# Attention feeding a four-expert MoE: x operands of a token group kept in SBUF for all experts, operand sums of the second product made in place just in time, chunks paired across token halves

## The chip, the cores and the metric

The kernel runs on one core of a Trainium2 chip, in fp32 throughout. The metric is device time in microseconds (us) of one execution. A few runs are timed, and one more execution is taken by the hardware profiler: the profile, the trace and all lines shown below come from that one execution.

## The reference

Lightning attention on q, k, v of shape (B=4, H=8, S=768, D=64), then a mixture of four experts over its output. Cut to what is computed:

```python
for b in range(nb):                      # blocks of 64 tokens
    intra = np.einsum('bhic,bhjc->bhij', qb, kb) * Dmask[None]
    intra = np.einsum('bhij,bhjd->bhid', intra, vb)
    inter = np.einsum('bhid,bhde->bhie', qb * lam_pow[None], kv_state)
    out[:, :, sl] = intra + inter
    kv_state = lam_block * kv_state + np.einsum('bhsd,bhse->bhde', kb * rev_pow, vb)
x = out.transpose(0, 2, 1, 3).reshape(B * S, H * D)         # [3072, 512]
p = domain_probs / (domain_probs.sum(-1, keepdims=True) + 1e-09)
for e in range(4):
    h = np.maximum(x @ w1[e], 0.0)                          # w1[e]: [512, 1024]
    out += p[:, e:e + 1] * (h @ w2[e])                      # w2[e]: [1024, 512]
```

## The kernel before, in words

**Tiles.** The 3072 tokens are cut into 24 chunks of 128 (a chunk is one batch row b and one stretch c of its sequence), eight chunks to a group, three groups (0, 1, 2) of 1024 tokens. A unit is a pair (group, expert), twelve in all. Chunks are worked on in pairs: attention for chunks n and n + 1 is done together, and in `where` (L110) the two chunks of a pair are neighbours in the group's order, so that a pair's 256 tokens lie in the same half of the group.

**The products.** Both matrix products of a unit use the Strassen-Winograd scheme on two levels. On each level a 2x2 block product is made from seven products M1 to M7 of sums of blocks: S1 to S4 are the sums on one side, T1 to T4 those on the other (`A_OF`, `B_OF`, L84 and L85). An outer product M of the first matrix product has seven inner products; for each the two operands are slices of tiles of [128, 7, 256], seven operands side by side: `ws` from w1 and `xs` from x. `first_product` (L862) issues them as matmuls at L884, adds the PSUM results on the vector engine (VectorE, DVE) or copies them on the scalar engine (ScalarE, ACT), and applies relu on ACT (L896). `second_product` (L923) multiplies the hidden blocks by tiles of w2 (L938), and DVE adds the gated result to the output accumulators (L951, L954). For the last group the second product is also nested on both levels (`nested_product` L1149, matmuls L1169). Group 0's first expert is made while attention for group 0 is still running, by `direct_product` (L1285, L1299).

**Order of the work.** The main loop (L1454 to L1527) runs over the units; for each, seven slots. Slot i interleaves the second product of M = `SEQ2[i]` of the present unit with the first product of M = `SEQ[i]` of the next unit (the list `order`, L1497), in eight steps x = 0 to 7. Slots are numbered 7 times the unit's position plus i. Everything else is put between these steps:

- `steps` are attention's pieces for groups 1 and 2, at slots given by the list `AT` (L641): loads two slots and one slot ahead, transposes on TensorE (L543) at the slot, scores (L570) at its end, the values (L606, L612, L620) at the end of the next one. L621 on copies a pair's output from PSUM (`op`) to `xT`, an SBUF tile that holds a whole group's x (ACT, L626).
- `chores` and `queue` are worked off by `pump` (L153). A chore is a piece of operand preparation on GpSimd (POOL); `tt` (L93) counts each POOL operation's size into a planned time `busy`, and `pump` starts the next chore when its planned start `free` has come. Stores of results wait in `queue` until the planned end of the sums. `until` (L173) pumps by force until something is made.
- `background` is a list of DVE sums, of which `rest` (L502) issues one after each step.

DMAs are issued almost all by SyncE (SP), whose queue is in order: an issue that waits holds all behind it. The tile framework adds the waits.

**The path of x.** When half of a group's chunks, or all of them, are in `xT`, `prepare_x` (L316) has POOL make the outer sums T1 to T4 and, for each of the seven M, `inner_x` (L205) makes four inner sums of 256 columns in a stage tile and stores the seven pieces in DRAM (`x_ops`, L185 to L187). `feed` (L789) then loads for each slot two tiles of 896 KB: `xs_in` (L797) from `x_ops` and `ws_in` (L799) from `w1_ops`; both tags of the pool `stream` have two buffers. So a group's x operands are loaded anew for each expert. For group 0 `own_x` (L1201) makes these sums on DVE, and the first use reads them from SBUF. `feed` stands at the first step of a slot (x = 0), from slot 6 on:

```python
        xs = stream.tile([P, 7, 256], FP32, name="xs_in", tag="x")
        nc.sync.dma_start(out=xs[:], in_=x_ops[g, MS.index(m)])
        ws = stream.tile([P, 7, 256], FP32, name="ws_in", tag="w")
        nc.sync.dma_start(out=ws[:], in_=w1_ops[e, MS.index(m)])
```

**The hidden sums.** When `first_product` has finished a quarter of the hidden blocks, `operands` (L672) puts its four sums S3, S1, S2, S4 into `background`, each into a new tile (`small`, a pool of `NPOOL` = 46 tiles of 2 KB per partition). In unit (0, 0) three blocks go through PSUM on the way (ACT copies, L689). `SEQ2` is M1, M2, M7, M6, M4, M5, M3, so S3 is read in the third slot, S2 in the fourth, S1 in the sixth and S4 in the seventh.

**Scaled q.** The states of attention, `kv`, are multiplied by q scaled with a decay (`qs`, DVE, L527 and L552), made beside qT.

Of the kernel before, what the change touches and what calls it, by code (L numbers as in the profile page):

```python
# [17 lines left out]
NPOOL = 46  # L18
# [3 lines left out]
def kernel(  # L22
# [36 lines left out]
    C = P  # L59
# [13 lines left out]
    stage = ctx.enter_context(tc.tile_pool(name="stage", bufs=8))  # L73
    w2pool = ctx.enter_context(tc.tile_pool(name="w2", bufs=6))
    stream = ctx.enter_context(tc.tile_pool(name="stream", bufs=2))
    opool = ctx.enter_context(tc.tile_pool(name="o", bufs=CPG))
# [13 lines left out]
    def small(name):  # L90
        return pool.tile([P, W], FP32, name=name, tag="t")

# [16 lines left out]

    def where(n):  # L110
        g, x = divmod(n, CPG)
        half, x = divmod(x, 4)
        return (2 * g + x // 2, 2 * half + x % 2) if g == LAST else (2 * g + half, x)

    def token(n):
        c, b = where(n)
        return b * S + c * C
# [3 lines left out]
    def load(n, names="qkv"):  # L121

        c, b = where(n)
        for name in names:
            x = small(f"{name}n")
# [12 lines left out]
    x_ops = dram.tile([NG, 7, P, 7, 256], FP32, name="x_ops")  # L138
# [4 lines left out]
    X_AT = {n: i for i, n in enumerate(("M1", "M7", "M6", "M4", "M5", "M2", "M3"))}  # L143
# [60 lines left out]

    def inner_x(eng, g, m, blk):  # L205
        at = {"B11": (0, 0), "B12": (0, 1), "B21": (1, 0), "B22": (1, 1)}
        inner(eng, ("x", g, m), x_ops[g, MS.index(m)], blk, T_OPS, at)
# [103 lines left out]
    xT = consts.tile([P, 4, G], FP32, name="xT")  # L311

    b11, b21 = xT[:, 0:2, 0:W], xT[:, 2:4, 0:W]
    b12, b22 = xT[:, 0:2, W:G], xT[:, 2:4, W:G]

    def prepare_x(g):  # L316

        st = {}

        def total(name, a, b, op):  # L320
            t = stage.tile([P, 2, W], FP32, name="xo", tag="st")
            halves(t[:], a, b, op)
            st[name] = t[:]

        def ready(m, blk):
            inner_x(nc.gpsimd, g, m, blk)

        return [lambda: ready("M1", b11), lambda: ready("M2", b21)], [
            lambda: total("T1", b12, b11, ALU.subtract), lambda: ready("M5", st["T1"]),
            lambda: total("T2", b22, st["T1"], ALU.subtract), lambda: ready("M6", st["T2"]),  # L330
            lambda: total("T3", b22, b12, ALU.subtract), lambda: ready("M7", st["T3"]),
            lambda: ready("M3", b22),
            lambda: total("T4", b21, st["T2"], ALU.subtract), lambda: ready("M4", st["T4"]),
        ]
# [1223 lines left out]
```

## Time and profile before

| What | us |
|---|---|
| median of 3 runs | 1196.85 |
| all runs | 1197.26, 1188.91, 1196.85 |
| the profiled execution | 1200.69 |
| its span (first to last instruction) | 1198.9 |
| mean granted TensorE clock in it | 0.996 |
| SyncE waits at xs_in issues (L797) for matmuls L884 | 128.8 in 31 waits |
| POOL x sums: outer (xo), 16 of 512 columns twice | 11.8 + 10.0 |
| ACT copies of op to xT (L626), 24 | 12.8 |
| ACT copies up at L689, 12 | 6.9 |
| DVE qs sums, 12 and 8 | 14.4 + 6.3 |

How to read the profile: a group of instructions is "line engine operation out<-in", with the names of tiles as the program has them and the shape; "x8" is a count of instruction records, and a 128x256 fp32 matmul has two of them. In a timeline, the bracket at the end of a row is the idle time before it and what ended it. "PEclk" is the TensorE clock that was granted, 1.00 is full. The DMA share is the mean busy share of the core's 16 DMA engines. A released wait is put down to the event that came last by the profile.

The busy time of an engine that is not the bottleneck, and its idle time, cost nothing by themselves. SyncE's waits in the table are of that sort as long as what it issues lands before its reader needs it.

### The profile page before, as it was taken

To read this page: it belongs to the slowest core of one execution; us is meant where nothing else is said; L and a number is where in the kernel's file an instruction comes from. 1 tells how busy PE (TensorE), PEld (TensorE's weight loads), DVE (VectorE), ACT (ScalarE), POOL (GpSimd) and SP (SyncE) were. 2 spreads that over 40 slices of the span, in tenths; PEclk is the share of its full clock that TensorE was granted. 3 is DMA by queue.
4 is the path that set the end of the run, shared out by engine and by line. 5 is a ranking of instruction groups with operands and counts; after the bars stand their busy time and mean duration, and the time that the engine had idled before them with its cause. 6 is when DMAs were issued, how large, how long until landed. Compare 5 with 4: busy or idle time off the path is not lost.

```text
span 1198.9 us, 17951 instructions
## 1 busy us (share of the span) xinstructions
PE 1175.7 (98%) x6559; PEld 1027.4 (86%) x6559; DVE 785.8 (66%) x1327; ACT 270.3 (23%) x476; POOL 632.1 (53%) x600
## 2 busy tenths in 40 slices
PE   8999999999999989999999999999999999999998
PEld 7888888888778878888888888888788888888887
DVE  4686795577358637756865864773565566776785
ACT  3332122112111201211120120121143352241331
POOL 2883167475338900045534272726575593683884
PEclk9999999999999999999999999999999999999999
DMA  9895969999999996799997989999987666657543
GB/s 222 230 327 178 273 227 289 354 351 319 313 328 345 325 300 198 230 293 307 309 325 259 279 295 314 290 299 310 310 267 274 228 235 238 240 214 264 204 158 96
DMA packets 266760, 324.25 MB, mean 270 GB/s; under 512 B 122640, under 2 KB 208048, under 8 KB 266672
## 3 DMA queue, kind: packets, MB, share of 16 engines
q1 hardware_dynamic: 256032, 320.28, 80.4%
q10 hardware_dynamic: 10640, 2.82, 1.1%
q8 instruction: 52, 0.85, 0.3%
q14 instruction: 36, 0.29, 0.1%
HBM read 237.69 MB, written 89.54 MB: 273 GB/s over the span
## 4 chain that ended last, share of the span: by engine, by line
PE 55%; DMA 1%; DVE 1%; ACT 0%; issue 0%; DVEq 0%; SPq 0%
PE pg L884 24%; PE q L938 15%; PE pq L1169 13%; DMA xs_in<-x_ops 1%; PE op L612 0%; DVE sums L94 0%; PE pg L1169 0%; PE sp L570 0%; PE pM L1105 0%; DMA w2b<-in_moe_w_dram 0%; PE op L606 0%; PE yp L1063 0%; PE yp L1138 0%; DVE y L1086 0%; DVE hS L94 0%; DVE st L94 0%
## 5 line engine op out<-in xcount | busy, mean ns | idle before, releaser
L884 PE MATMUL pg<-xs_in,ws_in 128*128 128x256 f32 x1960 | 474.0, 382 | 12.9 <-DMA ws_in<-w_ops 10.1
L884 PEld LDWEIGHTS pg<-xs_in,ws_in 128*128 128x128 f32 x1960 | 373.9, 191 | 67.3 <-issue 14.8
L94 DVE TENSOR_TENSOR m<-pg,m 128x512 f32<-128x512 f32 x451 | 307.8, 687 | 117.8 <-PE pg L884 110.9
L938 PE MATMUL q<-w2t,hS 128*128 128x256 f32 x1024 | 243.8, 381 | 0.0
L938 PEld LDWEIGHTS q<-w2t,hS 128*128 128x128 f32 x1024 | 194.6, 191 | 27.2 <-DMA w_ops<-w2b 0.2
L954 DVE SCALAR_TENSOR_TENSOR acc<-q,gate,acc 128x256 f32<-128x256 f32 x192 | 92.3, 481 | 147.6 <-PE q L938 146.6
L938 PE MATMUL q<-w2t,m 128*128 128x256 f32 x768 | 182.1, 380 | 0.0
L938 PEld LDWEIGHTS q<-w2t,m 128*128 128x128 f32 x768 | 145.4, 190 | 19.9
L896 ACT ACTIVATE m<-m 128x512 f32<-128x512 f32 x132 | 83.0, 630 | 296.6 <-DVE m L94 296.3
L94 POOL TENSOR_TENSOR m<-m,xT 128x512 f32<-128x512 f32 x64 | 80.6, 1274 | 69.8 <-ACT m L896 52.1
L94 POOL TENSOR_TENSOR ops<-w2b 128x256 f32<-128x256 f32 x24 | 19.2, 820 | 157.3 <-DMA w2b<-in_moe_w_dram 157.3
L892 ACT COPY m<-pg 128x512 f32<-128x512 f32 x88 | 51.5, 585 | 192.6 <-PE pg L884 192.4
L94 DVE TENSOR_TENSOR sums<-pq,sums 128x256 f32<-128x256 f32 x153 | 64.2, 421 | 46.1 <-PE pq L1169 38.9
L1169 PE MATMUL pq<-acc,w2t 128*128 128x256 f32 x352 | 86.6, 379 | 0.0
L1169 PEld LDWEIGHTS pq<-acc,w2t 128*128 128x128 f32 x352 | 66.9, 190 | 9.3 <-issue 0.3
L94 POOL TENSOR_TENSOR kn<-kn,s_decay 128x512 f32<-128x512 f32 x20 | 23.6, 1182 | 90.2 <-PE kp L543 38.8
L827 ACT ACTIVATE m<-m 128x512 f32<-128x512 f32 x44 | 27.7, 630 | 128.7 <-DVE m L94 128.7
L94 DVE TENSOR_TENSOR hS<-m,m 128x512 f32<-128x512 f32 x56 | 47.0, 839 | 14.7 <-ACT m L896 14.7
L94 POOL TENSOR_TENSOR acc<-hT,hT 128x512 f32<-128x512 f32 x32 | 40.2, 1271 | 30.3 <-PE pq L1169 28.4
L94 POOL TENSOR_TENSOR w2o<-w2b 128x512 f32<-128x512 f32 x32 | 42.7, 1355 | 25.4 <-DMA across<-in_q_dram 17.9
L94 POOL TENSOR_TENSOR ops<-w1o 128x256 f32<-128x256 f32 x32 | 27.8, 887 | 32.7 <-PE pg L884 17.3
L94 DVE TENSOR_TENSOR m<-m,m 128x512 f32<-128x512 f32 x56 | 44.9, 801 | 0.0
(159 smaller groups left out, 1351.3 us busy)
## 6 DMA issues: line engine op xcount, KB each, us to landing
xs_in<-x_ops SPq DMA_DIRECT2D x70, 896.0 KB, 6.1
ws_in<-w_ops SPq DMA_DIRECT2D x70, 896.0 KB, 8.4
w2t<-w_ops SPq DMA_DIRECT2D x66, 256.0 KB, 6.8
w2t<-w_sums SPq DMA_DIRECT2D x64, 256.0 KB, 4.0
w_ops<-ops SPq DMA_DIRECT2D x28, 512.0 KB, 4.4
w2t<-in_moe_w_dram SPq DMA_DIRECT2D x48, 256.0 KB, 3.7
w2b<-in_moe_w_dram SPq DMA_DIRECT2D x32, 256.0 KB, 6.2
w_sums<-w2o SPq DMA_DIRECT2D x16, 512.0 KB, 5.8
```

Of the source, the lines that this page charges most:

```text
L94: eng.tensor_tensor(out=o, in0=a, in1=b, op=op)
L827: nc.scalar.activation(out=o[:], in_=o[:], func=AF.Relu)
L884: nc.tensor.matmul(out=p[:, j * 256:(j + 1) * 256], lhsT=ws[i][:, j * P:(j + 1) * P], rhs=xs[i], start=(fresh and j == 0), stop=True, skip ...
L892: nc.scalar.copy(out=new[at][:], in_=p[:])
L896: nc.scalar.activation(out=new[at][:], in_=new[at][:], func=AF.Relu)
L938: nc.tensor.matmul(out=p[:, s * DH:(s + 1) * DH], lhsT=h[A_OF[m]][:, c * 256 + s * P:c * 256 + (s + 1) * P], rhs=fed2[g, e, m][uu][:, c], ...
L954: nc.vector.scalar_tensor_tensor(out=o, in0=x, scalar=w, in1=o, op0=ALU.mult, op1=ALU.add)
L1169: nc.tensor.matmul(out=p[:, 0:256], lhsT=fed3[e, m, x // 2][:, x % 2, c * P:(c + 1) * P], rhs=b[B_OF[i]][:, c * 256:(c + 1) * 256], start= ...
```

## The change

**x stays in SBUF.** There are seven fixed tiles of [128, 7, 256], one for each M, in a new pool `xp`. For group 0 the attention's values are copied straight into them, and DVE makes the inner sums in place (`x_steps`). For groups 1 and 2 ACT copies a pair's output into one stage tile, POOL makes the four outer sums of the pair (`pair_sums`), and SyncE stores the pair's seven blocks in DRAM (`x_blocks`, two stores of 384 and 512 KB). Later `x_fill` loads the blocks into the seven tiles, one M per slot from slot 18 (group 1) and slot 43 (group 2), by two DMAs of 256 KB each, and a chore makes the inner sums on POOL, in place. `feed` loads only `ws_in`. `x_ops` is gone, as are `prepare_x` and `inner_x`.

**Chunks paired across halves.** So that a pair's outer sums can be made alone, `where` puts the two chunks of a pair into the two halves of the group. The output rows of a chunk pair of the last group are then 256 neighbouring tokens, and the final stores are written accordingly: `give_across` issues four DMAs after the first half and four after the second, where before all eight followed the second.

**Hidden sums in place.** `operands` queues only S3, which takes the place of A21. `later_operands`, called at the start of each slot, queues S2 in the slot of M4 (in place of S3), S1 in the slot of M2 (in place of A11) and S4 in the slot of M5 (in place of A12). `SEQ2` becomes M1, M7, M4, M6, M2, M5, M3. The copies through PSUM of unit (0, 0) are gone.

**Room and places.** q is scaled in place after the scores (in group 0 on DVE right behind the four masks). `kv` and `q_decay` come from the pool of small tiles and are given back when the last attention is done (`forget`); `gate_bc` lies in `s_decay`; in group 0 the k tiles come from the accumulators' pool and the v tiles from that of w2. `NPOOL` is 41 for 46, the stage pool has 7 tiles for 8. The end weights `w2s` of the nested products take six different x tiles. The list `AT` is 7, 10, 13, 15, 22, 27, 32, 37 for 4, 8, 13, 17, 24, 29, 34, 39. The matmuls are the same in number and shapes.

The diff, cut to its core:

```diff
-NPOOL = 46
+NPOOL = 41
...
-    stage = ctx.enter_context(tc.tile_pool(name="stage", bufs=8))
+    stage = ctx.enter_context(tc.tile_pool(name="stage", bufs=7))
     w2pool = ctx.enter_context(tc.tile_pool(name="w2", bufs=6))
     stream = ctx.enter_context(tc.tile_pool(name="stream", bufs=2))
+    xp = ctx.enter_context(tc.tile_pool(name="xp", bufs=1))
...
+    def token(g, half, x):
+        c, b = (half, x) if g == 0 else (2 * g + x % 2, 2 * (x // 2) + half)
+        return b * S + c * C
+
+    def where_of(n):
+        return n // CPG, n % CPG // 4, n % 4
+
     def where(n):
         g, x = divmod(n, CPG)
-        half, x = divmod(x, 4)
-        return (2 * g + x // 2, 2 * half + x % 2) if g == LAST else (2 * g + half, x)
-
-    def token(n):
-        c, b = where(n)
-        return b * S + c * C
+        return (x // 4, x % 4) if g == 0 else (2 * g + x // 2 % 2, 2 * (x // 4) + x % 2)
...
-    def inner_x(eng, g, m, blk):
-        at = {"B11": (0, 0), "B12": (0, 1), "B21": (1, 0), "B22": (1, 1)}
-        inner(eng, ("x", g, m), x_ops[g, MS.index(m)], blk, T_OPS, at)
...
-    xT = consts.tile([P, 4, G], FP32, name="xT")
-    b11, b21 = xT[:, 0:2, 0:W], xT[:, 2:4, 0:W]
-    b12, b22 = xT[:, 0:2, W:G], xT[:, 2:4, W:G]
-    def prepare_x(g):
-        st = {}
-        def total(name, a, b, op):
-            t = stage.tile([P, 2, W], FP32, name="xo", tag="st")
-            halves(t[:], a, b, op)
-            st[name] = t[:]
-        def ready(m, blk):
-            inner_x(nc.gpsimd, g, m, blk)
-        return [lambda: ready("M1", b11), lambda: ready("M2", b21)], [
-            lambda: total("T1", b12, b11, ALU.subtract), lambda: ready("M5", st["T1"]),
-            lambda: total("T2", b22, st["T1"], ALU.subtract), lambda: ready("M6", st["T2"]),
-            lambda: total("T3", b22, b12, ALU.subtract), lambda: ready("M7", st["T3"]),
-            lambda: ready("M3", b22),
-            lambda: total("T4", b21, st["T2"], ALU.subtract), lambda: ready("M4", st["T4"]),
+    slots = {m: xp.tile([P, 7, 256], FP32, name="xs", tag="x" + m) for m in MS}
+    def whole(t):
+        return t[:, 0:4].rearrange("p (c a) f -> p c (a f)", c=2)
+    def x_steps(g, m, eng):
+        t = slots[m]
+        return [
+            lambda o=o, x=x, y=y: tt(eng, t[:, o], t[:, x], t[:, y], ALU.subtract)
+            for o, x, y in ((4, 3, 1), (1, 1, 0), (5, 3, 1), (6, 2, 5))
         ]
+    def x_inner(g, m):
+        for f in x_steps(g, m, nc.gpsimd):
+            f()
+        made.add(("x", g, m))
+    def x_fill(g, m):
+        for x in range(4):
+            until(("blocks", g, x))
+        slots[m] = xp.tile([P, 7, 256], FP32, name="xs", tag="x" + m)
+        for a in range(2):
+            nc.sync.dma_start(
+                out=whole(slots[m])[:, a].rearrange("p (x t) -> p x t", x=4),
+                in_=x_blocks[g - 1, :, :, BLOCK_AT[m], a * C:(a + 1) * C],
+            )
+        chores.insert(0, lambda: x_inner(g, m))
...
-        masks = []
+        masks, scale = [], []
         for m, pair in zip((n, n + 1), tags):
-            qT, kT, scaled[m] = turned.pop(m)
+            qT, kT = turned.pop(m)
+            scaled[m] = qT
             sp = [bank(pair[r], "sp") for r in range(2)]
             for ac in range(NHP):
                 for r in range(2):
@@ -571,19 +582,24 @@
                         out=sp[r][:, ac * C:(ac + 1) * C], lhsT=hc(kT)[half[r], ac], rhs=hc(qT)[half[r], ac],
                         start=True, stop=True,
                     )
+            del kT
             st = masked[m] = [small("st") for _ in range(2)]
             def mask(hd, st=st, sp=sp):
                 tt(nc.vector, st[hd][:], sp[hd][:], s_decay[:, hd].rearrange("p h c -> p (h c)"), ALU.mult)
             masks.append([lambda hd=hd, mask=mask: mask(hd) for hd in range(2)])
+            if where(m)[0]:
+                scale.append(lambda qT=qT: tt(nc.vector, qT[:], qT[:], decay["q"][:], ALU.mult))
         if n < CPG:
-            for f in masks[0] + masks[1]:
+            for f in masks[0] + masks[1] + scale:
                 f()
         else:
             for f in masks[1]:
                 f()
-            soon(n, *masks[0])
+            soon(n, *masks[0], *scale)
...
-        at = n % CPG * C
-        for r in range(2):
-            nc.scalar.copy(
-                out=xT[:, 2 * r:2 * r + 2, at:at + 2 * C], in_=op[r][:].rearrange("p (a t) -> p a t", a=2),
-            )
+        g, x = divmod(n, CPG)
+        if g == 0:
+            at = x % 4 * C
+            for r, to in enumerate((slots["M1"], slots["M2"]) if x < 4 else (b12[0], slots["M3"])):
+                nc.scalar.copy(out=whole(to)[:, :, at:at + 2 * C], in_=op[r][:].rearrange("p (a t) -> p a t", a=2))
+        else:
+            o = stage.tile([P, 4, 256], FP32, name="xc", tag="st")
+            for r in range(2):
+                nc.scalar.copy(
+                    out=o[:, 2 * r:2 * r + 2].rearrange("p s (a t) -> p a s t", a=2),
+                    in_=op[r][:].rearrange("p (a s t) -> p a s t", a=2, s=2),
+                )
+            chores.insert(0, lambda: pair_sums(g, x // 2, o))
...
+    def pair_sums(g, x, o):
+        s = stage.tile([P, 4, 256], FP32, name="to", tag="st")
+        b12, b11, b22, b21 = (o[:, i] for i in range(4))
+        for to, a, b in ((0, b12, b11), (1, b22, s[:, 0]), (2, b22, b12), (3, b21, s[:, 1])):
+            tt(nc.gpsimd, s[:, to], a, b, ALU.subtract)
+        store(lambda: (
+            nc.sync.dma_start(out=x_blocks[g - 1, :, x, 0:3], in_=o[:, 1:4]),
+            nc.sync.dma_start(out=x_blocks[g - 1, :, x, 3:7], in_=s[:]),
+            made.add(("blocks", g, x)),
+        ))
+    AT = 7, 10, 13, 15, 22, 27, 32, 37
+    FILL = {1: 18, 2: 43}
...
-        def total(name, a, b, op, drop=()):
-            def step():
-                o = small("h" + name)
-                tt(nc.vector, o[:], h[a][:], h[b][:], op)
-                h[name] = o
-                for x in drop:
-                    del h[x]
-            return step
-        if key[:2] == (0, 0):
-            def bring(name, tag):
-                there[name] = bank(tag, "up")
-                nc.scalar.copy(out=there[name][:], in_=h[name][:])
-            def step(name, a, b, op, drop=(), then=None):
-                def f():
-                    o = small("h" + name)
-                    tt(nc.vector, o[:], there.get(a, h[a])[:], there.get(b, h[b])[:], op)
-                    h[name] = o
-                    for x in drop:
-                        del h[x]
-                    if then:
-                        bring(*then)
-                return f
-            there = {}
-            background.extend([
-                lambda: bring("A21", "s0"), step("S3", "A11", "A21", ALU.subtract, (), ("A11", "s1")),
-                step("S1", "A21", "A22", ALU.add, ("A21",)), step("S2", "S1", "A11", ALU.subtract, (), ("A12", "s0")),
-                step("S4", "A12", "S2", ALU.subtract),
-            ])
-            return
-        background.extend([
-            total("S3", "A11", "A21", ALU.subtract), total("S1", "A21", "A22", ALU.add, ("A21",)),
-            total("S2", "S1", "A11", ALU.subtract), total("S4", "A12", "S2", ALU.subtract),
-        ])
+        def step():
+            t = h["S3"] = h.pop("A21")
+            tt(nc.vector, t[:], h["A11"][:], t[:], ALU.subtract)
+        background.append(step)
+    def later_operands(g, e, m):
+        def step(h, a):
+            if m == "M4":
+                t = h["S2"] = h.pop("S3")
+                tt(nc.vector, t[:], a[:], t[:], ALU.subtract)
+            elif m == "M2":
+                t = h["S1"] = h.pop("A11")
+                tt(nc.vector, t[:], h["S2"][:], t[:], ALU.add)
+            else:
+                t = h["S4"] = h.pop("A12")
+                tt(nc.vector, t[:], t[:], h.pop("S2")[:], ALU.subtract)
+        if m in ("M4", "M2", "M5"):
+            for sj in (1, 0):
+                for uu in range(2):
+                    h = hid[g, e, uu, sj]
+                    background.append(lambda h=h, a=h["A22"] if m == "M4" else None: step(h, a))
...
-        if (g, e, m) in fed:
-            return
-        while ("x", g, m) not in made and background:
-            rest(force=True)
-        until(("x", g, m))
         until(("w1", e, m))
-        xs = stream.tile([P, 7, 256], FP32, name="xs_in", tag="x")
-        nc.sync.dma_start(out=xs[:], in_=x_ops[g, MS.index(m)])
         ws = stream.tile([P, 7, 256], FP32, name="ws_in", tag="w")
         nc.sync.dma_start(out=ws[:], in_=w1_ops[e, MS.index(m)])
-        fed[g, e, m] = {i: xs[:, X_AT[i]] for i in X_AT}, {i: ws[:, W1_AT[i]] for i in W1_AT}
+        fed[g, e, m] = {i: ws[:, W1_AT[i]] for i in W1_AT}
...
-    SEQ2 = ("M1", "M2", "M7", "M6", "M4", "M5", "M3")
+    SEQ2 = ("M1", "M7", "M4", "M6", "M2", "M5", "M3")
...
-                t = stream.tile([P, 7, 256], FP32, name="w2s", tag="xw"[SEQ3.index(m) % 2])
+                t = xp.tile([P, 7, 256], FP32, name="w2s", tag="x" + SEQ[SEQ3.index(m)])
...
-        for x in range(2):
-            at = (2 * x + t) * P
-            nc.vector.transpose(out=o[:, at:at + P], in_=sums[m][:, 2 * dd + t, x * P:(x + 1) * P])
-        d = i * DH + dd * P
-        for a in range(4 * t):
+        nc.vector.transpose(out=o[:, t * 256:(t + 1) * 256], in_=sums[m][:, 2 * dd + t])
+        r, d = token(LAST, j, 2 * t), i * DH + dd * P
+        for a in range(4):
             by = nc.scalar if a == 1 else nc.sync
-            for x in range(2):
-                to = by_batch[2 * j + x, 2 * LAST * C:, d + a * 32:d + (a + 1) * 32].rearrange("(q p) d -> p q d", p=32)
-                of = o[a * 32:(a + 1) * 32, 2 * x * P:2 * (x + 1) * P]
-                by.dma_start(out=to, in_=of.rearrange("p (q d) -> p q d", d=32))
+            by.dma_start(
+                out=out[r:r + 256, d + a * 32:d + (a + 1) * 32].rearrange("(b p) d -> p b d", p=32),
+                in_=o[a * 32:(a + 1) * 32, t * 256:(t + 1) * 256].rearrange("p (b d) -> p b d", d=32),
+            )
...
+        if at == 6:
+            forget()
...
+            if (g, e) < (LAST, 0):
+                later_operands(g, e, SEQ2[i])
...
+                for h in range(1, NG):
+                    if x == 3 and 0 <= at * 7 + i - FILL[h] < 7:
+                        x_fill(h, SEQ[at * 7 + i - FILL[h]])
```

## The prediction

> **What bounds the kernel now.** I read first the busy table and the slices of the page, then the stretches in windows, then TensorE alone in time, then the DMA issues. From the page:
>
> ```profile
> PE 1175.7 (98%) x6559; PEld 1027.4 (86%) x6559; DVE 785.8 (66%) x1327; ACT 270.3 (23%) x476; POOL 632.1 (53%) x600
> DMA  9895969999999996799997989999987666657543
> GB/s 222 230 327 178 273 227 289 354 351 319 313 328 345 325 300 198 230 293 307 309 325 259 279 295 314 290 299 310 310 267 274 228 235 238 240 214 264 204 158 96
> ```
>
> TensorE is busy 98% of the span; nothing else is above 66%, but the DMA engines are full for most of 210 to 450 us. So the end is the sum of TensorE's work and its few gaps, and only the gaps can be won: the matmuls stay the same, shape by shape (2476 of 128x256 in both programs). The work has a clear beat. Eight matmul records of a slot start 1.73 us after the eight before them (216 ns each), and a slot without attention lasts 12.95 us. I listed the slots' starts from TensorE's timeline and looked where one is longer than its kind. Windows around those places, with two undisturbed ones (columns: length, PE, PEld, DVE, ACT, POOL busy, clock, DMA share, GB/s):
>
> ```profile
> 330.00:360.00 30.00, 27.47 (x150) 23.58 (x149) 16.59 (x26) 4.55 (x8) 11.68 (x12) 0.94 0.99 330
> 420.00:450.00 30.00, 25.40 (x116) 22.01 (x115) 11.98 (x20) 1.54 (x3) 1.95 (x3) 0.98 0.91 300
> 820.00:850.00 30.00, 27.39 (x121) 23.63 (x120) 14.80 (x25) 3.09 (x6) 12.34 (x15) 0.94 0.92 306
> 850.00:880.00 30.00, 30.00 (x141) 26.43 (x140) 17.96 (x30) 8.83 (x15) 23.30 (x24) 1.00 0.96 317
> 1000.00:1030.00 30.00, 30.00 (x141) 26.44 (x140) 21.00 (x39) 5.39 (x9) 10.59 (x9) 1.00 0.61 221
> ```
>
> In the first three TensorE lacks 2.5 to 4.6 us and the clock dips; in the others it is full, at a DMA share of 0.96 as at 0.61. TensorE's timeline gives the gaps (start, length, and in brackets the idle time before and what ended it):
>
> ```profile
> 327.22 1.96 PE L884 MATMUL pg<-xs_in,ws_in 128*128 128x256 f32 x8 [2.44 <-DMA ws_in<-w_ops]
> 342.94 3.42 PE L884 MATMUL pg<-xs_in,ws_in 128*128 128x256 f32 x8 [2.53 <-DMA ws_in<-w_ops]
> 448.52 3.19 PE L884 MATMUL pg<-xs_in,ws_in 128*128 128x256 f32 x8 [4.60 <-DMA ws_in<-w_ops]
> 842.09 3.42 PE L884 MATMUL pg<-xs_in,ws_in 128*128 128x256 f32 x8 [2.61 <-DMA w2b<-in_moe_w_dram]
> 845.35 1.89 PE L938 MATMUL q<-w2t,hS 128*128 128x256 f32 x8
> ```
>
> All four are first products at the start of a slot, waiting for their streamed operands. The fourth names a w2b load, but the chain of waits has "828.25 10.55 DMA xs_in<-x_ops" before it: SyncE issued xs_in at 828.25, then waited 4.5 us (for the gate_rows load) before it could issue ws_in at 833.28. After a gap the next eight matmuls take 3.2 to 3.4 us in three of the four, where eight in the beat take 1.89. What they wait for, by the page (issues, KB each, median us to landing):
>
> ```profile
> xs_in<-x_ops SPq DMA_DIRECT2D x70, 896.0 KB, 6.1
> ws_in<-w_ops SPq DMA_DIRECT2D x70, 896.0 KB, 8.4
> ```
>
> **What the Trainium skill says.** "TensorE: Matmul & The Clock Gate" (section "What's actually happening") has the array at half rate after an idle window of about 3.4 us. The trace agrees in kind, 3.42 against 1.89 us for eight matmuls and a clock of 0.94 over 30 us; it differs in that gaps of 2.5 us were enough. "DMA: Bandwidth & Descriptors" ("Issuing engines are not separate DMA queues") says that all DMAs share the same 16 engines and interleave; the trace agrees, since ws_in, issued behind an equal xs_in, lands 2.3 us later in the median and 9 us after its issue at 317.92. "SBUF — State Buffer" ("Who interferes with whom") lets DVE and GpSimd contend for one port pair; the DVE sums with a PSUM source (m<-pg,m) take 687 ns, those from SBUF alone (hS<-m,m) 839.
>
> **The change, part by part.** The account is that of the profiled execution: 1200.69 us = span 1198.90 + 1.79 around it. It lies 3.8 above the median of the runs (1196.85); one run of the same program took 1188.91, so some 8 us of gaps come and go by themselves.
>
> Removed, x reloads: 70 x 896 KiB, 64.2 MB; and the stores of x sums, 21 x 896 KiB, 19.3 MB. Added: stores of x blocks, 8 x 896 KiB, 7.3 MB, and fills, 14 x 512 KiB, 7.3 MB. Net -68.8 MB of 324.25, or -21%, and 90 fewer of SyncE's 1050 issues, at about 0.4 us each. At each slot's start ws_in no longer follows an equal transfer. What that is worth on the path are the four slots: 15.63 us against 12.95 (2.7), 21.31 against 16.78 for one with such attention (4.5), 21.63 against 15.1 (6.5), 17.25 against 12.95 (4.3): 18.0 us, of which 12.2 is idle (2.44 + 2.53 + 4.60 + 2.61) and the rest slow matmuls. The clock says the same: 30 x (0.06 + 0.06 + 0.04 + 0.02) = 5.4. Would they go? The worst, before 448.52, was late by 4.6 us with 896 KB ahead of it, which at the window's 300 GB/s is 3.1 us, and its issue moves up by the 0.4 us that xs_in's took. I leave the other 1.0 us as still there; bounds 0 and 10. Smaller excesses (under 1 us each, 2 us in all, around 158 and 277 us) sit where DMA or DVE is full; half of them: -1.0.
>
> The fills: each waits in SyncE's queue for the blocks' stores, and ws_in is behind it. Group 1's last values are at the end of slot 16, the sums take 4 x 0.85 us on POOL, and the fill stands in slot 18, over 13 us on; stores take 4 to 8 us. The old operand was last read four slots earlier (one for group 2). The inner sums have two slots or more, so no gap: 0, bounds 0 and +4. POOL has 16 sums more (610 for 594, 14 us on an engine at 53%): 0.
>
> The hidden sums: 128 as before (112 of them 0.77 to 0.84 us, from SBUF; the 16 of unit (0,0) lose their PSUM source), now in place, S2, S1 and S4 each one slot before its reader. DVE is fullest in slot 5: 11.88 us of a 12.95 us slot at 262.30. In the built program 12 to 14 matmul records lie between the last S4 and its reader, 2.6 to 3.0 us; less one sum of 0.8 leaves about 2. DVE's lag behind TensorE in before's slots is mostly under 0.04 us and up to 0.75 at slots' starts. So seven of eight units cost nothing. In the last unit before the nested products only 4 to 8 records lie between (0.86 to 1.7 us): +0.5. Bounds 0 and the 8 x 4 us of rival (c). Behind S4 on DVE stand first-product sums, whose PSUM banks TensorE would wait for.
>
> qT scaled in place: in the start (L606 at 41.09 and 50.99) the scaling now stands between the masks and the product that reads it: 2 x 0.8 to 1.2 us on DVE twice, some of it under other matmuls; the x sums of M1 (4 x 0.55 us) leave DVE there. I take +1.0; bounds -1 and +3. Later in the kernel it has a slot's time: 0.
>
> ACT: 12 copies of 588 ns fewer, off the path at 23% busy: 0. Its copies into xc need a stage buffer, of which there are 7 for 8; five of them follow stores issued 8 to 14 us earlier, which take 4 to 8. Behind a late one stand the PSUM copies of a first product. 0; bounds 0 and +4. The end (output stores of 256 tokens, half of the last issued earlier): TensorE ends at 1195.74, so at most 1 us of 3.1: 0. The 2.0 us gap before the turn of the gates at 510.95 stays.
>
> Sum of the span: 1198.9 - 18.0 + 1.0 - 1.0 + 0.5 + 1.0 = 1182.4; with 1.8 around it 1184.2. The 3.8 by which this execution lies above the median are either more of the same gaps, which the sum has already removed, or the profiler's, which come off in full; I can't tell and take half off: 1182.
>
> **The rivals.** (a) The gaps go only in part, 0.20. Attention's q, k and v loads keep SyncE 4 us at a time (the v issue at 323.00 took 3.98), weight preparation still writes and reads 28 + 28 + 56 pieces, and SyncE can still be held in front of ws_in as at 828.25. For it: two of the gaps are within 20 us of that v load. Against: 90 issues fewer, and the v load stood behind ws_in. Half of 18 stays: 1182 + 8 = 1190. (b) The transfers were hidden anyway, and what falls away in those four places comes back elsewhere, 0.08: for it, the two windows of a full TensorE at DMA shares of 0.96 and 0.61, and that the moved attention (slots 7 to 16 in place of 4 to 18) puts its loads closer together; 1196. (c) The other side, 0.07: the just-in-time sums come late in each of the eight units. DVE in slot 5 is full, at 262.30 it has 1.1 us to spare, and one attention step there pushes S4 past its reader; TensorE waits and runs slowly after. It cancels the gain at 15 / 8, about 1.9 us a unit, and passes the 1% bound from 3.4 us a unit: 4 us each (2.5 idle, 1.5 slow) give 1182 + 32 = 1214. Against it: the 0.75 us lag. (d) More is won (the small excesses, the gate turn), 0.05: 1177.
>
> **How the numbers follow.** The likeliest case (0.60) is 1182, its own range 1178 to 1187. With (a), (b) and (d) the range is 1176 to 1196; outside it stay (c) and the edges. A measurement of this kernel can tell about 1% from no change: 1184.9 and 1208.8. The likeliest lies mostly below 1184.9 (0.54 of 0.60), with (d) and some of (a) 0.63; (c) is 0.07; between them 0.30.
>
> **What would show it.** Right: no row of TensorE's waits names ws_in over 1 us; no clock below 0.98 in a 30 us window before 1150; DMA near 255 MB; ws_in landing in 4 to 6 us; the beat still 1.73. Wrong: L938 matmuls waiting for DVE on a tile S4 at the end of a unit (c); gaps at L884 that name fills, v loads or stores (a); ACT idle before xc on a DMA, with L884 waiting behind it.

## The result

Over 20 runs each the changed kernel took 1193.49 us (1188.54 to 1196.93) and the kernel before 1196.85 us (1188.66 to 1199.97): ratio 0.998, 95% interval 0.9963 to 0.9996. It is 2.4 us faster by the ratio (3.4 between the medians), where the prediction had 15. The profiled execution took 1194.33 us with a span of 1192.5, against 1200.69 and 1198.9.

The page of the changed kernel, with the rows that answer to those shown of before (busy time, DMA share and rate in 40 slices, the ws_in loads):

```profile
PE 1172.8 (98%) x6559; PEld 1024.5 (86%) x6559; DVE 788.5 (66%) x1323; ACT 263.8 (22%) x464; POOL 634.6 (53%) x616
DMA  9685578958896976659868656776774535444442
GB/s 232 191 256 186 160 228 277 284 191 273 268 351 215 288 244 211 198 181 284 262 208 251 211 191 211 252 245 209 242 237 167 178 132 186 141 158 169 144 183 71
ws_in<-w_ops SPq DMA_DIRECT2D x70, 896.0 KB, 6.4
```

The traffic went as forecast: 255.42 MB for 324.25, and ws_in lands in 6.4 us for 8.4. But slice 12 still shows 351 GB/s, and TensorE has a dent there. The windows of the changed kernel at the three bad places of before (columns as in the prediction):

```profile
330.00:360.00 30.00, 23.97 (x180) 20.19 (x179) 20.56 (x29) 1.07 (x2) 15.80 (x15) 0.94 0.98 349
420.00:450.00 30.00, 29.85 (x200) 25.59 (x200) 20.55 (x34) 2.58 (x5) 11.73 (x14) 1.00 0.78 246
820.00:850.00 30.00, 30.00 (x141) 26.41 (x140) 19.51 (x33) 5.39 (x9) 13.98 (x16) 1.00 0.76 243
```

The gaps at 448 and 842 us are gone. The stretch from 330 us is worse than before: TensorE lacks 6.0 us where it lacked 2.5. TensorE's timeline names the gaps of over 1 us behind the start (start, length, idle before and its end in brackets):

```profile
255.70 1.99 PE L899 MATMUL pg<-xs,ws_in 128*128 128x256 f32 x8 [1.48 <-DVE m L101]
...
333.82 3.56 PE L899 MATMUL pg<-xs,ws_in 128*128 128x256 f32 x8 [3.21 <-DMA ws_in<-w_ops]
...
345.38 1.99 PE L899 MATMUL pg<-xs,ws_in 128*128 128x256 f32 x8 [2.82 <-DVE m L101]
...
509.79 0.27 PE L491 MATMUL gp<-ident,gn 128*32 128x128 f32 x1 [1.84 <-DVE gn L490]
```

One gap for ws_in is left, though xs_in no longer runs ahead of it, and two for DVE are new. Why ws_in is late is in SyncE's timeline (changed kernel, all rows of the stretch):

```profile
245.26 0.34 SPq L812 DMA_DIRECT2D ws_in<-w_ops  x1
260.94 0.92 SPq L142 DMA_DIRECT2D qn<-in_q_dram  x2
```

From 245.60 to 260.94 SyncE issues nothing. Its waits in the window from 244 to 300 us (total, times, longest):

```profile
SPq L142 <- PE op L625: 8.1, 1, 8.1
SPq L142 <- DVE qT L101: 7.2, 1, 7.2
```

It stands at a q load of attention, 7.2 us until DVE has scaled a qT and 8.1 us more until the values of the pair before (L625) have read theirs: the load has no tile to write into before that, as the experiments below bear out. I then took for each ws_in its issue, its landing and the first matmul that reads it, all from the trace. "Lead" is issue to reader, "margin" landing to reader, in us; the slot is the one in which the load is issued, and its first reader stands at the start of the next:

```
slot        before         changed        one load moved (a_load13)
           lead margin    lead margin    lead margin
 11         9.3   1.5     20.6  14.2     19.8  12.9
 12         8.4   0.1      8.8   1.1     18.5  13.5
 13         9.2   0.2      8.7   0.1     17.4  10.0
 14        10.5   1.0      8.6   0.5     19.0  11.4
 15         9.3   0.1      7.5   0.1     15.2   9.1
 16         8.3   0.1     17.9   9.7     20.7  13.7
```

The changed kernel is 11 us better off than before at slot 11, the load stands, and for four slots ws_in is as late as it was. Over all 70 loads the reader came within 0.2 us of the landing seven times before and twice after.

### The profile page after: what moved, and what is told of

It reads as the page before. It is cut to its first block, busy times and chain, and to the rows that moved or that the text cites. A ratio compares the mean times of both kernels' runs of the same rounds, so it can differ in the third digit from the quotient of the medians.

```text
span 1192.5 us, 17848 instructions
## 1 busy us (share of the span) xinstructions
PE 1172.8 (98%) x6559; PEld 1024.5 (86%) x6559; DVE 788.5 (66%) x1323; ACT 263.8 (22%) x464; POOL 634.6 (53%) x616
## 2 busy tenths in 40 slices
DMA packets 264551, 255.42 MB, mean 214 GB/s; under 512 B 121200, under 2 KB 218256, under 8 KB 264464
## 3 DMA queue, kind: packets, MB, share of 16 engines
q10 hardware_dynamic: 10640, 2.82, 1.0%
## 4 chain that ended last, share of the span: by engine, by line
PE 89%; DVE 7%; DMA 2%; POOL 1%; issue 0%; ACT 0%; SPq 0%; DVEq 0%; POOLq 0%
PE pg L899 37%; PE q L953 29%; PE pq L1179 13%; DVE m L101 3%; PE pM L1274 2%; PE op L631 2%; PE pc L1274 2%; DMA ws_in<-w_ops 1%; PE sp L581 1%; DVE st L101 1%; DVE qT L101 1%; PE op L625 1%; PE kvp L639 1%; POOL acc L101 0%; POOL m L101 0%
## 5 line engine op out<-in xcount | busy, mean ns | idle before, releaser
L899 PE MATMUL pg<-xs,ws_in 128*128 128x256 f32 x1960 | 471.4, 381 | 9.0 <-DVE m L101 4.9
L899 PEld LDWEIGHTS pg<-xs,ws_in 128*128 128x128 f32 x1960 | 372.1, 191 | 63.2 <-DVE m L101 8.4
L953 PE MATMUL q<-w2t,m 128*128 128x256 f32 x1792 | 425.3, 380 | 0.0
L953 PEld LDWEIGHTS q<-w2t,m 128*128 128x128 f32 x1792 | 338.8, 190 | 47.5 <-DVE m L101 0.4
L101 DVE TENSOR_TENSOR m<-m,m 128x512 f32<-128x512 f32 x184 | 151.7, 824 | 9.8 <-ACT m L911 9.8
L101 POOL TENSOR_TENSOR m<-m,s_decay 128x512 f32<-128x512 f32 x64 | 81.9, 1297 | 58.7 <-ACT m L911 45.5
L101 POOL TENSOR_TENSOR xs<-xs 128x256 f32<-128x256 f32 x56 | 44.2, 789 | 86.6 <-DMA xs<-x_blocks 70.7
L101 POOL TENSOR_TENSOR to<-xc 128x256 f32<-128x256 f32 x16 | 13.2, 825 | 129.1 <-ACT xc L651 91.1
L101 POOL TENSOR_TENSOR w2o<-w2b 128x512 f32<-128x512 f32 x32 | 41.9, 1330 | 37.0 <-DMA w_sums<-w2o 18.6
L101 POOL TENSOR_TENSOR acc<-hT,acc 128x512 f32<-128x512 f32 x32 | 40.7, 1272 | 7.7 <-PE pq L1179 5.7
L101 DVE TENSOR_TENSOR st<-sp,s_decay 128x512 f32<-128x512 f32 x48 | 30.4, 682 | 17.8 <-PE sp L581 17.8
L101 POOL TENSOR_TENSOR w1o<-w1b 128x512 f32<-128x512 f32 x20 | 27.5, 1400 | 22.5 <-DMA w_ops<-ops 9.9
```

The costliest lines, as they stand in the source:

```text
L101: eng.tensor_tensor(out=o, in0=a, in1=b, op=op)
L899: nc.tensor.matmul(out=p[:, j * 256:(j + 1) * 256], lhsT=ws[i][:, j * P:(j + 1) * P], rhs=xs[i], start=(fresh and j == 0), stop=True, skip ...
L953: nc.tensor.matmul(out=p[:, s * DH:(s + 1) * DH], lhsT=h[A_OF[m]][:, c * 256 + s * P:c * 256 + (s + 1) * P], rhs=fed2[g, e, m][uu][:, c], ...
```

## The experiments

All ratios are to the kernel before, run on the same chip, with 95% intervals. Kernels on the base of before are named b_ or x_ (xs_ for one), those on the changed kernel a_ or l_.

**Loads taken away, sums alone, another queue.** b_xs_once leaves out 69 of the 70 loads of xs_in:

```diff
-        xs = stream.tile([P, 7, 256], FP32, name="xs_in", tag="x")
-        nc.sync.dma_start(out=xs[:], in_=x_ops[g, MS.index(m)])
+        if not once:
+            once.append(stream.tile([P, 7, 256], FP32, name="xs_in", tag="x"))
+            nc.sync.dma_start(out=once[0][:], in_=x_ops[g, MS.index(m)])
+        xs = once[0]
```

> The kernel before, but one x operand tile is loaded once and read by every first product in place of the 70 loads of xs_in (so the first products multiply the wrong x; nothing else is left out, the x sums and their stores stay). Theory T (traffic: ws_in is late because xs_in takes the DMA engines, and what the whole change gained was given back on DVE): the gaps at L884 go and the time falls by 12 to 18 us, to 1179 to 1185. Theory Q (SyncE's in-order queue: ws_in is issued too late, behind attention loads and weight preparation, so that less traffic helps little): 2 to 6 us, 1191 to 1195. Theory H (transfers hidden anyway): within 2 us of before.

Measured 1184.97 us, 0.9892 (0.9862 to 0.9922), span 1183.6. The three windows of this kernel have no gap left:

```profile
330.00:360.00 30.00, 30.00 (x169) 26.15 (x169) 22.96 (x36) 4.56 (x8) 18.84 (x18) 1.00 0.88 285
420.00:450.00 30.00, 30.00 (x156) 26.29 (x157) 19.66 (x34) 2.87 (x5) 2.12 (x2) 1.00 0.79 234
820.00:850.00 30.00, 30.00 (x141) 26.41 (x140) 18.10 (x31) 4.81 (x8) 15.38 (x19) 1.00 0.85 280
```

The time is the one that theory T forecast: every gap for ws_in is gone, at 261 MB of traffic, about that of the changed kernel. So the gain exists, and something else in the change gives most of it back. The run does not separate theories T and Q, since 69 issues leave SyncE's queue together with their traffic. For the loads issued in slots 12 to 16, ws_in landed 6.3 to 8.1 us after its issue, for 8.2 to 9.5 before; but its lead rose to 14.5 to 20.9 us, from 8.3 to 10.5. Most of what these loads won is an earlier issue. The four bad places of the kernel before are likewise places of a short lead (8.3 to 9.4 us, where the median of the 70 loads is 13.2), and not of a slow landing (8.2 to 9.3 us, median 8.4).

b_jit takes `operands`, `later_operands` and `SEQ2` from the changed kernel, with nothing else:

```diff
-    SEQ2 = ("M1", "M2", "M7", "M6", "M4", "M5", "M3")
+    SEQ2 = ("M1", "M7", "M4", "M6", "M2", "M5", "M3")
...
+            if (g, e) < (LAST, 0):
+                later_operands(g, e, SEQ2[i])
```

> The kernel before with only the hidden sums changed: in place, S3 at once, S2, S1 and S4 one slot before their readers, the new order of second products, no copies through PSUM in unit (0, 0). Theory T (gain given back on DVE): DVE is late in attention slots, 4 to 8 us slower than before, 1201 to 1205. Theory Q: within 2 us of before, since the queue's delay is untouched. The forecast's own step: +0.5 us.

Measured 1195.0 us, 0.9982 (0.9963 to 1.0001): the sums in place show no cost here.

b_ws_act and a_ws_act move one issue:

```diff
-        nc.sync.dma_start(out=ws[:], in_=w1_ops[e, MS.index(m)])
+        nc.scalar.dma_start(out=ws[:], in_=w1_ops[e, MS.index(m)])
```

> The kernel before with the ws_in loads issued by ScalarE in place of SyncE. Theory Q: ws_in goes out a slot ahead whatever stands in SyncE's queue, the gaps at L884 go, 8 to 15 us faster, 1182 to 1189. Theory T: the traffic is the same, within 3 us of before; some loss if ScalarE's copies wait behind the issue.

> The changed kernel with the ws_in loads issued by ScalarE in place of SyncE. Theory Q: the gap of 3.2 us at L899 that names ws_in goes with its slow matmuls (some 5 us), 1187 to 1189. Theory T: the gaps that name DVE stay and are most of the loss, 1190 to 1193.5.

Measured 1.0045 (1.0029 to 1.006) and 0.9973 (0.9959 to 0.9988). On the base the gain that theory Q forecast did not come, but this is no clean test of it: ws_in now had margins of 3 to 9 us at slots 12 to 17, while xs_in, still on SyncE, had become the late one (its reader came within 0.3 us of the landing eight times, with a gap of 4.12 us before 448.35 us), and on balance the kernel is slower; what on ScalarE makes it so was not followed further. On the changed kernel the gap for ws_in went (margins of 5 to 10 us at slots 12 to 15), but a gap of 1.64 us for an ACT copy came at 320.78 and one of 1.39 us for DVE at 442.23, and the 2.80 us for DVE stayed. Giving the late load another queue removed its wait and gained nothing clear (0.9973, where the changed kernel has 0.998).

**What gives it back: three parts on top of the base without reloads.** x_at has `AT` = 7, 10, 13, 15, 22, 27, 32, 37; x_jit the sums of b_jit; x_scale scales q in place after the masks:

```diff
+            if where(m)[0]:
+                scale.append(lambda qT=qT: tt(nc.vector, qT[:], qT[:], q_decay[:].rearrange("p h c -> p (h c)"), ALU.mult))
...
-            soon(n, *masks[0])
+            soon(n, *masks[0], *scale)
```

> The kernel before with one x operand tile loaded once (as in b_xs_once, the first products multiply the wrong x) and with the changed kernel's list of attention slots, 7, 10, 13, 15, 22, 27, 32, 37. The base took 0.989 of before. Theory A (the closer attention of group 1 fills DVE and SyncE's queue there and takes the gain back): 0.994 to 0.997, with gaps between 240 and 350 us. Theory S (the late scaling of q) and theory J (the just-in-time sums): 0.989.

> The kernel before with one x operand tile loaded once (wrong x) and the hidden sums in place and just in time. Theory J: the sums come late once the transfers no longer hide it, 0.993 to 0.997 of before, with gaps that name DVE. Theories A and S: 0.989, since the sums alone left the kernel before where it was (0.998).

> The kernel before with one x operand tile loaded once (wrong x) and q scaled in place after the masks. Theory S: 0.992 to 0.996 of before, with gaps that name DVE in the slots of the values and in the start. Theories A and J: 0.989 to 0.990 (some 1 us in the start).

> The kernel before with one x operand tile loaded once (wrong x) and all three: the list of attention slots, the just-in-time sums, the late scaling of q. If these three together are what took the gain back: 0.996 to 0.999 of before, with the gaps of the changed kernel at 254 and 342 us. If it is something else (the new path of x over POOL and its stores, fewer buffers): 0.989 to 0.992.

Measured: x_at 0.9916 (0.9892 to 0.9939), x_jit 0.9881 (0.9859 to 0.9904), x_scale 0.9927 (0.9904 to 0.995), all three 0.9926 (0.9902 to 0.9949). Theory J falls a second time. The attention slots and the scaling may cost 3 to 4 us each, though each interval overlaps the base's 0.9892; x_all has a gap of 1.98 us for DVE near 259 us, as the changed kernel has at 255.70. But at 0.9926 it is well below the changed kernel's 0.998, with no gap at 330 us: the larger part was elsewhere.

**The load that stands.** a_load13 moves one load step, that of the pair at slot 13, past the values that free its tiles; a_load moves all of them:

```diff
-            steps.append((at - 2, 1, lambda n=n: load_more(n)))
+            steps.append((at - 1, 0, lambda n=n: load_more(n)) if at == 13 else (at - 2, 1, lambda n=n: load_more(n)))
```

> The changed kernel with one thing moved: the q, k and v loads of the first chunk of the pair at slot 13 go into the program at the start of slot 12 in place of slot 11. Theory B (buffers: with 41 small tiles for 46 these loads find no free tile until the values of the pair before, SyncE stands for 15.7 us at 245 us, and every ws_in of the four slots after goes out only some 8.7 us ahead of its use): SyncE does not stand there, the leads at slots 12 to 15 are 13 us or more, the gap of 3.2 us at 330 us is gone with its slow matmuls, 0.993 to 0.995 of before. Theory D (DVE alone): 0.997 to 0.998 as the changed kernel.

> The changed kernel with all loads of attention in groups 1 and 2 put later: the pair's first chunk at the start, its second in the middle of the slot before the transposes, in place of two slots and one slot before. Theory B: as with the one load moved, 0.992 to 0.995 of before, unless a load now lands after the transposes want it (then gaps at the transposes). Theory D: 0.997 to 0.998.

Measured 1186.84 us, 0.9907 (0.9876 to 0.9938), and 1188.65 us, 0.9922 (0.9894 to 0.9951). SyncE's timeline of a_load13 over the same stretch:

```profile
247.56 0.34 SPq L812 DMA_DIRECT2D ws_in<-w_ops  x1
248.81 2.14 SPq L385 DMA_DIRECT2D across<-in_k_dram  x3
251.00 0.59 SPq L195 DMA_DIRECT2D w_ops<-w1b  x1
...
260.04 1.25 SPq L934 DMA_DIRECT2D w2t<-in_moe_w_dram  x2
261.77 0.34 SPq L812 DMA_DIRECT2D ws_in<-w_ops  x1
262.40 0.92 SPq L142 DMA_DIRECT2D qn<-in_q_dram  x2
```

What stood behind the q load (weight pieces, w2t, ws_in) now goes out before it; the leads are in the table above, and there is no gap at 330 us:

```profile
330.00:360.00 30.00, 30.00 (x218) 26.35 (x217) 22.27 (x38) 2.96 (x5) 15.97 (x17) 1.00 0.67 231
```

Theory B holds: one step moved, 7.0 us between the profiled spans, 6.7 between the medians (8.7 by the two ratios). It is an edit of program order alone, with the same instructions. The DMA engines are not full in this window either (share 0.67 for 0.98), so their load there came of the stand and was not its cause.

The gap of 2.82 us for DVE is gone too, although the scaling of q stands where it stood. In the changed kernel, what came late included loads for GpSimd, whose sums then fell beside those of DVE; here GpSimd is idle in that stretch (the rows are in the last section). Slot 16 as a whole takes 17.01 us for 25.14. Of these 8.1 us, 3.21 were the wait for ws_in, 1.6 the slow matmuls behind it and 2.82 the wait for DVE.

Is it the number of small tiles? x_np41 and xs_np38 put fewer into x_all:

```diff
-NPOOL = 46
+NPOOL = 41
```

> The kernel before with one x operand tile loaded once (wrong x), the attention slots, the just-in-time sums and the late scaling (that took 0.9926 of before), and now 41 small tiles in place of 46. Theory B: the loads stand for tiles and ws_in becomes late, 0.996 to 0.999 of before. Theory D, or the new path of x as the cause: 0.992 to 0.993.

> The base with one x operand tile loaded once (wrong x), attention slots, just-in-time sums and late scaling, with 38 small tiles (46 took 0.9926 of before, 41 took 0.991). Theory B, shortage alone: SyncE stands at a q, k or v load for over 8 us, the lead of ws_in falls under 9 us, 0.995 to 0.999. If the order of releases in the changed kernel is needed too: 0.990 to 0.993.

41 gave 0.991 (0.9882 to 0.9938), no cost; theory B as first put missed. In the changed kernel `kv` (two tiles) and `q_decay` (one) come from that pool too, so 38 is the like number, and it gave 1193.22 us, 0.9965 (0.9953 to 0.9977). The traces agree. SyncE and TensorE of xs_np38, which has the old path of x:

```profile
245.93 0.34 SPq L785 DMA_DIRECT2D ws_in<-w_ops  x1
265.67 0.92 SPq L133 DMA_DIRECT2D qn<-in_q_dram  x2
```

```profile
339.17 3.32 PE L870 MATMUL pg<-xs_in,ws_in 128*128 128x256 f32 x7 [3.50 <-DMA ws_in<-w_ops]
```

A stand of 19.4 us at the same load, leads of 7.4 to 8.5 us at slots 12 to 14 and of 6.6 at slot 15, whose reader waits 3.50 us. In x_all, with the same 260.93 MB of traffic, the leads at slots 12 to 15 are 13.3 to 18.6 us, and there is no wait for ws_in. So on top of x_all fewer small tiles alone bring the stand and the late ws_in, and a loss (0.9965 for 0.9926; the intervals do not overlap). The new stores, fills and sums of x are not needed for it, nor is the smaller stage pool, which has 8 tiles here.

**What is left.** a_scale_pool puts the scaling of q for groups 1 and 2 on GpSimd, in the changed kernel; l_gates takes a_load13 and issues the eight copies of the gates one chore before their transpose; l_gates_pool adds the GpSimd scaling; l_gates_s1 instead makes S1 one slot earlier:

```diff
-                scale.append(lambda qT=qT: tt(nc.vector, qT[:], qT[:], decay["q"][:], ALU.mult))
+                scale.append(lambda qT=qT: tt(nc.vector if n < CPG else nc.gpsimd, qT[:], qT[:], decay["q"][:], ALU.mult))
...
-                chores.append(turn_gates)
+                chores.extend((line_gates, turn_gates))
...
-            elif m == "M2":
+            elif m == "M6":
                 t = h["S1"] = h.pop("A11")
```

> The changed kernel with the in-place scaling of q for groups 1 and 2 done by GpSimd in place of DVE. Theory D (DVE is too full in the slots of attention's values): the gaps of 1.5 and 2.8 us that name DVE shrink to under 1, 0.994 to 0.996 of before. Theory B: those gaps shrink too, but the gap for ws_in stays, 0.996 to 0.998; if GpSimd stands at a full stage pool, the values wait for it and it is slower.

> The changed kernel with the one load moved to slot 12 (0.9907 of before by itself) and the eight copies of the gates issued one chore ahead of their transpose. The gap of 1.8 us before the transpose at 500 us goes: 2 us less, 0.989.

> The one load moved, the gates one chore ahead, and the scaling of q for groups 1 and 2 on GpSimd. If DVE in the slots of values is the rest of the loss: 0.986 to 0.988. If GpSimd, held at its stage buffers, brings the scaled q late (it did at 306 us in the run with the scaling alone): 0.989 to 0.992.

> The one load moved, the gates one chore ahead, and S1 made one slot earlier (in the slot of M6 in place of that of M2), which takes four sums out of slot 11, where DVE is fullest. If DVE's load in that slot is what the gap of 2 us at 255 us is: that gap goes, 0.986 to 0.988; if port contention with GpSimd or the order is: it stays, 0.989.

a_scale_pool: 0.9957 (0.9944 to 0.9971). The two gaps for DVE went, and one for GpSimd came; the stand of SyncE stayed, 12.7 us. TensorE's timeline of a_scale_pool:

```profile
310.24 2.36 PE L625 MATMUL op<-qT,kv 64*64 64x128 f32 x32 [3.32 <-POOL qT L101]
```

l_gates: 1185.05 us, 0.9898 (0.9876 to 0.992). l_gates_pool and l_gates_s1: 1183.17 us each, 0.9884 (0.9862 to 0.9906) and 0.9881 (0.9859 to 0.9903). TensorE's waits for DVE sums, first of l_gates, then of l_gates_s1:

```profile
PE pg L903 <- DVE m L101: 2.3, 3, 1.8
```

```profile
PE pg L903 <- DVE m L101: 1.4, 2, 1.2
```

With S1 a slot earlier the gap near 256 us is gone: it was the load of DVE in slot 11. The 1.2 us that are left are a gap at 434.39 us, where l_gates has none and a_load13 has 1.21 us at 436.61. Both versions beat the kernel before and the changed one. Their time is near the 1182 of the prediction for the change itself, with the help of the gap at the gates, which the prediction had left in.

## Why the prediction was wrong, point by point

**What bounds the kernel: right in place and worth, half right in the reason.** The ends of the gaps were named rightly, and so was their worth: b_xs_once, which takes away loads and their issues, gained 15.3 us of span in the profiled executions (1198.9 to 1183.6), against 18.0 less 1.0 in the account. 1182 can nearly be had with this change: 1183.17. The reason given was the equal transfer ahead of ws_in. The leads say that the late issue weighed more, and xs_np38 shows that less traffic alone does not save a load that is issued late.

**Transfers: right.** 255.42 MB against 255.5 from the terms of the account. What the Trainium skill says in "TensorE: Matmul & The Clock Gate" ("What's actually happening"), half rate after an idle window of about 3.4 us, fits again in kind: behind the gap of 3.21 us eight matmuls took 3.56 us, clock 0.94 in that window; behind that of 2.82 us they took 1.99. Its "DMA: Bandwidth & Descriptors" ("Issuing engines are not separate DMA queues") fits too: in the changed kernel ws_in landed 6.6 us after its issue in the median when ScalarE issued it, and 6.4 when SyncE did.

**The step that failed** is "I leave the other 1.0 us as still there". The account asked what runs ahead of ws_in on the DMA engines, and not when SyncE gets to issue it. The parts list names the stage pool's buffer (7 for 8) and never the five small tiles (41 for 46) nor the three that kv and q_decay take of the rest. Thirty-eight for 46 makes a q load stand 15.3 us in the one in-order queue that carries almost everything. The 90 issues fewer, which the prediction held against rival (a), were no protection: a queue that stands delays all, however short it is. The runs show the term: not 1.0 but some 7 to 9 us, which is what a_load13 returns (spans 1192.5 to 1185.5; ratios 0.998 to 0.9907). The term's upper bound, 10, would have held it. Rival (a) had the right mechanism, "SyncE can still be held in front of ws_in", with a chance of 0.20, but looked for its cause in the loads' length, 3.98 us, and not in a tile that is not free.

The nearest number, 1196, is rival (b)'s. Its first half, that the transfers were hidden anyway, is refuted by b_xs_once; its second, that what falls away comes back elsewhere, is what happened. Of the reasons given for it, attention's loads lying closer together comes near, but tiles are not named. That 1193.49 lies between 1176 and 1196 is thus luck: the gain that was forecast did not come.

**"Later in the kernel it has a slot's time: 0"**, on the scaling of q, was wrong by a smaller amount. Two sums on DVE moved from the turn to the slot of the values, where four hidden sums may also stand. In slot 11, of 19.0 us, the lengths of DVE's instructions add up to 17.29 us, and TensorE waits 1.48 us. That it is these sums together with S1 is shown by l_gates_s1 and l_gates_pool, from which the gap is gone; the size of the whole effect, 2 us in the medians, is near the noise (ranges of runs 1184.84 to 1185.54 for l_gates, 1182.71 to 1184.88 for l_gates_pool and 1182.27 to 1183.75 for l_gates_s1). The gap of 2.82 us in slot 16 needed both faults: it went when the scaling left DVE (a_scale_pool), and it went when only the load was moved (a_load13), where the same 23 instructions of DVE add up to 15.07 us in place of 18.71.

Of the 10.1 us by which the profiled span missed the sum (1192.5 for 1182.4), the moved load returns 7.0, and S1 one slot earlier 1.5 more (1183.1 in l_gates, 1181.6 in l_gates_s1; each is one execution). The other 1.6 are not assigned.

**The just-in-time sums: right.** +0.5 us forecast. Two runs found no cost (0.9982 and 0.9881, against 1 and 0.9892), so rival (c) is out. At the place that the forecast named, the last unit before the nested products, TensorE waited 0.55 us for DVE in x_jit, and in the changed kernel the seventh slot's first eight matmuls took 2.19 us for 1.89.

**The start: right in kind.** TensorE waits 1.4 us for qT, but the first slot begins at 90.0 us, as before at 90.1; +1.0 was 1 us too much.

**The gates** cost 1.84 us, about as foreseen, and l_gates shows that they need not. **ACT and POOL:** the xc copies once waited 6.9 us and the pair sums 38 us in all, by the profile for DMAs, without a gap of TensorE at either: 0 was right.

**Open:** how much of b_xs_once's gain is the traffic and how much the shorter queue; and whether the closer attention slots cost anything by themselves (x_at 0.9916 against 0.9892, intervals overlapping). The old slots with the smaller pool of small tiles were not tried, so the stand is shown for the new slots only.

## What to carry to other kernels

Memory that keeps data on chip is taken from something: list every pool that gets smaller or gains a tenant, and ask for each whose next tile is released by what, and what queue its writer stands in. A DMA issue that waits for a buffer holds every later issue of its queue (here for 15.3 us), so the price is paid by another transfer, slots later; look at lead (issue to reader) and not only at landing time. When a gain fails to come, take the gain's cause alone, then add the other parts back one by one; and ask of each such kernel what else it takes away, as b_xs_once took issues along with the traffic.

## What the runs showed of the hardware

In these traces the time of a DVE sum from SBUF alone depends strongly on GpSimd. In the changed kernel such a sum took 0.68 us at 331.05, with GpSimd idle; 7 us later, DVE's rows, and below them those of GpSimd:

```profile
338.02 1.68 DVE L101 TENSOR_TENSOR m<-m,m 128x512 f32<-128x512 f32 x1
339.62 1.75 DVE L101 TENSOR_TENSOR qT<-qT,q_decay 128x512 f32<-128x512 f32 x1
341.30 0.47 DVE L969 SCALAR_TENSOR_TENSOR acc<-q,gate,acc 128x256 f32<-128x256 f32 x1
341.69 1.36 DVE L101 TENSOR_TENSOR m<-m,m 128x512 f32<-128x512 f32 x1
342.98 1.75 DVE L101 TENSOR_TENSOR qT<-qT,q_decay 128x512 f32<-128x512 f32 x1
```

```profile
336.66 2.49 POOL L101 TENSOR_TENSOR w2o<-w2b 128x512 f32<-128x512 f32 x2 [6.39 <-DMA w2b<-in_moe_w_dram]
339.11 6.73 POOL L101 TENSOR_TENSOR w2o<-w2b,w2o 128x512 f32<-128x512 f32 x4
```

They took 1.36 to 1.75 us, up to 2.6 times as long, and the accumulation with a PSUM source between them took its usual 0.47. GpSimd's own sums took 1.25 to 1.7 us there. In a_load13 the same two scalings come at a time when GpSimd has no work (its row names an idle time of 12.23 us before 345.94); DVE first, then GpSimd:

```profile
334.90 0.68 DVE L101 TENSOR_TENSOR qT<-qT,q_decay 128x512 f32<-128x512 f32 x1
336.49 0.68 DVE L101 TENSOR_TENSOR qT<-qT,q_decay 128x512 f32<-128x512 f32 x1
```

```profile
345.94 0.73 POOL L101 TENSOR_TENSOR to<-xc 128x256 f32<-128x256 f32 x1 [12.23 <-ACT xc L651]
```

These two and the two m<-m,m beside them take 2.7 us here; the four rows of the changed kernel take 6.5 us, 3.8 more, and its gap there is 2.82 us. This agrees with what the Trainium skill says in "SBUF — State Buffer" ("Who interferes with whom"): a DVE instruction with two SBUF inputs contends with a GpSimd instruction that reads SBUF. The mean of 0.8 us used in the account hid it.
